# Two pools instead of one behind the attention, other low words on GpSimd, and another port rule and other priorities in the planner

## Chip, cores and metric

The kernel runs on one core of one Trainium2 chip. The metric is the device time of one execution in microseconds (us): the median of several runs. An engine is named as in the profile: PE is TensorE, DVE VectorE, ACT ScalarE, POOL GpSimd, SP the queue that issues most DMAs.

## What is computed

```python
# q, k, v: (4, 8, 768, 64); proj (64, 6)
bucket = sum(((x @ proj) > 0) * 2**j)            # of every q row and k row
scores = where(q_bucket == k_bucket, 0.125 * q @ k.T, -1e9)
attn   = exp(scores - max) ; attn /= attn.sum + 1e-9 ; out = attn @ v
x = out with the 8 heads side by side             # (4, 768, 512)
h = gelu(x @ w_in)                                # (4, 768, 1024), tanh form
u, v = h[..., :512], h[..., 512:]
v_n = (v - mean) / sqrt(var + 1e-6) * g_ln
v_s = w_sg @ v_n + b_sg
out = x + (u * v_s) @ w_out
```

The weights w_in, w_sg and w_out come as 64-bit floats; the kernel makes 32-bit words of them. All large products run as three matmuls over a high and a low word of each factor.

## The kernel before

**Attention.** Sixteen pairs (a batch and two heads) are worked through in halves of 384 queries, 32 halves in all. `prepare` transposes q and k and makes the bucket features (PE lines 491 and 511, DVE 498 and 514). `largest` computes scores for the row maxima (PE L531), which DVE reduces (`mx`, L536, six reductions to a half); `shift` brings the maxima into the features. `weigh` computes the scores again (PE L569), ACT takes the exponentials into a ring of eight tiles `p` (L573), and POOL adds them up into `sum` (L586, ten additions of 128x384 to a half). `weighted` multiplies them with v (PE L597, 24 matmuls). `finish` sends the sums through four small DMAs to get reciprocals, scales, and stores the half's x to DRAM (`xs`).

**Input weights.** `weight_job` turns a piece of 128x256 of w_in into words: one POOL product (L369), and on DVE the operations of lines 367, 368, 370, 372, 373, 374, then an ACT copy (L375) and a DVE subtraction (L376). Sixteen such jobs are spread over the attention, by the priority `WSTEP * i + WP`. The same function makes the output weights `woh`, `wol` later, in sixteen pieces of 128x128 with one set of buffers (`ow`, `owx`, `owy`, `owg`).

**The gMLP.** For each batch: `load_x` fetches x and splits it (ACT L700, POOL L698). `hidden_v` is 72 matmuls (L765) into six PSUM banks, a gelu on ACT and DVE (L749, L750, L752, L754), the norm (L772 to L775), the scaling (L777), the high word `zh` on ACT (L779) and the low word `zl` on DVE (L781); its result `y` has two buffers. `hidden_u` is 96 matmuls (L797) and a gelu. `gate` is 144 matmuls (L815), then L818, L822, L823 and on POOL L826. `project` is 72 matmuls (L841) and a transpose for the residual (L846). Batch 0's `hidden_v` runs inside the last attention halves. Between batch 0's `hidden_u` and its `gate`, the gate weights are loaded on the ACT queue (b_sg at L707, six loads of w_sg at L716, 384 KB each), transposed on PE (L724), and split on ACT (L730) and DVE (L733).

**What sets the order.** `Plan` collects all operations with a cost and a priority and works out an order by a list schedule over engines, PSUM banks and DMA lanes; `run` then emits the instructions in that order, and each engine takes its own in order. Its `port` rule holds back operations of DVE and POOL that are marked as users of a shared port: after one starts, none of either engine is planned before its end. Memory comes from pools on a left and a right stack. Left are `late`, `odd`, `even`, `early` (attention). `b3` on the right (gate weights, output weights, `u`, `gs`, and the small tiles `gt`, `rx`, `ob`) is opened when all four are closed, the finishing steps of the last half among them.

Of the kernel before, what the change touches and what calls it, by code (L numbers as in the profile page):

```python
# [9 lines left out]
F32 = mybir.dt.float32  # L10
F32R = mybir.dt.float32r
# [10 lines left out]
MLP = {"xl": "POOL", "gm": "DVE", "gl": "POOL", "wg": 434.12, "wo": 12.91, "x": 469.98}  # L22

HID = 260.1
AVP = 2.39
S0P = 1.18
AHEAD = 4
PREP, SHIFTP, FINP, WSTEP, WP = 5.65, -1.32, 4.0, 37.92, -61.79
# [4 lines left out]
class Plan:  # L33
# [5 lines left out]
    WAIT = 0.2  # L39
    SOON = 0.11  # L40
# [38 lines left out]
    def add(self, engine, cost, prio, fn, r=(), w=(), dma=0, port=None, form=None, lat=0.0):  # L79
# [4 lines left out]
        for kind, xs in (("r", r), ("w", w)):  # L84
            for x in xs:
# [23 lines left out]
    def order(self):  # L109
# [14 lines left out]
        port, form = 0.0, None  # L124

        def since(n):
            e = G[n]["e"]
            if G[n]["dma"]:
                return max(seq.get(e, 0.0), lanes[-self.LANES] if len(lanes) >= self.LANES else 0.0)
            return max(free[e], seq.get(e, 0.0), port if G[n]["port"] and not G[n]["dma"] else 0.0)  # L130
# [11 lines left out]
        while len(out) < len(G):  # L142
# [53 lines left out]
            else:  # L196
                free[e] = end
                if g["port"]:
                    port = end
# [32 lines left out]
def kernel(  # L232
# [103 lines left out]
    def weight_job(plan, tile_of, src, c, f0, CW, th, tl, fac, prio):  # L336
# [14 lines left out]
        ops = iter(range(1, 12))  # L351

        def when():
            i = next(ops)
            return prio

        def vec(fn, r, wr):
            plan.add("DVE", 0.07 + CW / 960.0, when(), fn, r, wr, port=True)

        def vec2(fn, r, wr):  # L360
            plan.add("DVE", 0.07 + CW / 1920.0, when(), fn, r, wr, port=True)

# [4 lines left out]
        vec2(lambda: V.tensor_scalar(y(), hi(), 3, 0x3FFFFFFF, op0=ALU.logical_shift_left, op1=ALU.bitwise_and), [w], [y])  # L367
        vec(lambda: sts(x(), hi(), -0x40000000, y(), op0=ALU.bitwise_and, op1=ALU.bitwise_or), [w, y], [x])  # L368
        plan.add("POOL", 0.14 + CW / 512, when(), lambda: nc.gpsimd.tensor_mul(g(), hi().bitcast(F32), hi().bitcast(F32)), [w], [g])  # L369
        vec(lambda: sts(xf(), g(), LEAST * LEAST, xf(), op0=ALU.is_ge, op1=ALU.mult), [x, g], [x])  # L370

        vec2(lambda: V.tensor_single_scalar(y(), x(), -0x800000, op=ALU.bitwise_and), [x], [y])
        vec(lambda: sts(yf(), lo().bitcast(U32), 2.0 ** -52, yf(), op0=ALU.mult, op1=ALU.mult), [w, y], [y])
        vec(lambda: V.tensor_add(xf(), xf(), yf()), [x, y], [x])
        plan.add("ACT", 0.06 + CW / 1300, when(), lambda: nc.scalar.mul(part(th), xf(), fac), [x], [d] + bufs[:1])  # L375
        vec(lambda: sts(part(tl), xf(), fac, part(th).bitcast(F32), op0=ALU.mult, op1=ALU.subtract),  # L376
            [x, d] + bufs[:1], bufs[1:])
# [5 lines left out]
    MEM = "MEM"  # L383
    xd = [[plan.buf(f"xd_{b}_{c}", 1) for c in range(NC)] for b in range(B)]
# [36 lines left out]
    late, odd, even, early = (Pool(n, "left") for n in ("late", "odd", "even", "early"))  # L421
# [7 lines left out]
    if True:  # L429
# [22 lines left out]
        ptiles = [late.pool.tile([P, 2, SH + 1], F32, tag=f"p{i}", name=f"p{i}", bufs=1) for i in range(NPT)]  # L452
# [3 lines left out]
        def p_tile():  # L456
            late.list.append(plan.buf("p", NPT, lambda i: ptiles[i % NPT]))
            return late.list[-1]
# [450 lines left out]
```

## Time and profile before

| | us |
|---|---|
| median of 3 runs | 815.61 |
| lowest, highest | 812.11, 815.83 |
| the profiled execution, its own time | 815.91 |
| its span, first to last instruction | 814.1 |

A busy PE in the profile is a PE with a matmul in its pipeline. Waits are put down to what released them last. The granted clock of PE is 1.00 at 2.4 GHz and 0.50 at 1.2 GHz; a number between is a mean over a stretch. Instruction shapes are partitions x elements.

### The profile page before, as it was taken

What the parts mean: (1) busy time and instruction counts of PE and PEld (TensorE: products, weight loads), DVE (VectorE), ACT (ScalarE), POOL (GpSimd) and SP (SyncE); (2) the same over time, 40 slices, a digit from 0 to 9 for tenths busy, and PEclk for the clock granted to TensorE, in tenths of its full rate; (3) what the DMA queues carried; (4) which work ended last, traced back from release to release, by engine and by line L of the source; (5) the groups of instructions that cost most, each with busy time, mean ns of one, the idle gap of its engine ahead of it and who ended that gap; (6) DMA issues with size and microseconds to landing.
All of it is one profiled execution on the core that took longest, in us unless ns stands there. A gap on an engine that the chain in (4) does not pass through costs nothing.

```text
span 814.1 us, 14589 instructions
## 1 busy us (share of the span) xinstructions
PE 772.9 (95%) x5480; PEld 614.5 (75%) x5480; DVE 553.7 (68%) x918; ACT 403.5 (50%) x702; POOL 427.9 (53%) x466
## 2 busy tenths in 40 slices
PE   4979999999999999999999999599899999999998
PEld 3657667776767676776767669489898889988996
DVE  7986876877668769779677556698982158407730
ACT  2345656666566556665666565524432136214411
POOL 1465878787887777877877753233232202401130
PEclk9989999999999999999999999799999999999999
DMA  8003441432244224313311011610124220030003
GB/s 206 15 27 80 121 105 53 125 98 67 84 110 103 69 54 115 89 46 101 89 42 40 31 30 51 219 46 20 46 73 153 93 66 20 21 128 28 1 0 130
DMA packets 99302, 60.89 MB, mean 75 GB/s; under 512 B 64288, under 2 KB 91040, under 8 KB 99232
## 3 DMA queue, kind: packets, MB, share of 16 engines
q1 hardware_dynamic: 97920, 56.94, 25.3%
q10 hardware_dynamic: 1312, 3.02, 1.1%
q8 instruction: 43, 0.70, 0.4%
q14 instruction: 27, 0.22, 0.1%
HBM read 47.16 MB, written 12.78 MB: 74 GB/s over the span
## 4 chain that ended last, share of the span: by engine, by line
PE 80%; DVE 14%; DMA 2%; issue 2%; ACT 1%; POOL 0%; SPq 0%; ACTq 0%; DVEq 0%
PE psb L597 15%; PE psb L569 14%; PE psb L815 10%; PE psb L841 8%; PE psb L531 8%; PE psb L765 7%; PE psb L797 6%; PE psb L511 4%; DVE mx L536 4%; PE psb L491 3%; PE psb L612 1%; PE psb L846 1%; PE psb L549 1%; DVE wy L367 1%; DVE owx L368 1%
## 5 line engine op out<-in xcount | busy, mean ns | idle before, releaser
L586 POOL TENSOR_TENSOR sum<-sum,p 128x384 f32<-128x384 f32 x256 | 239.8, 969 | 10.6 <-ACT p L573 10.6
L536 DVE TENSOR_REDUCE mx<-psb 128x2 f32<-128x768 f32 x192 | 174.1, 949 | 62.3 <-PE psb L531 59.0
L573 ACT ACTIVATE p<-psb 128x768 f32<-128x768 f32 x192 | 146.5, 812 | 71.6 <-PE psb L569 68.5
L597 PE MATMUL psb<-p,v 128*64 128x385 f32 x768 | 133.5, 498 | 0.0
L597 PEld LDWEIGHTS psb<-p,v 128*64 128x64 f32 x768 | 52.9, 138 | 64.8 <-issue 62.0
L586 POOL TENSOR_TENSOR sum<-p,p 128x384 f32<-128x384 f32 x64 | 64.1, 1022 | 36.9 <-ACT p L573 36.6
L531 PE MATMUL psb<-fk,fq 64*128 64x384 f32 x384 | 72.8, 374 | 4.5 <-DVE mx L536 1.7
L569 PE MATMUL psb<-hq,hk 64*128 64x384 f32 x384 | 69.6, 356 | 5.3 <-DVE mx L536 4.6
L750 DVE SCALAR_TENSOR_TENSOR h<-h,psb 128x384 f32<-128x384 f32 (+1 forms) x56 | 32.6, 604 | 60.8 <-ACT h L749 60.6
L826 POOL TENSOR_TENSOR gs<-gt,gs 128x384 fp32r<-128x384 f32 x32 | 33.5, 1052 | 76.2 <-ACT gs L823 75.8
L775 POOL TENSOR_TENSOR mv<-mv,epsr 128x1 f32<-128x1 f32 x24 | 14.1, 587 | 106.0 <-DVE mv L774 101.1
L815 PE MATMUL psb<-wgh,zh 128*128 128x384 f32 x192 | 65.3, 340 | 4.4 <-DVE u L754 3.0
L841 PE MATMUL psb<-woh,gs 128*128 128x512 f32 x192 | 65.5, 402 | 0.0
L531 PE MATMUL psb<-hk,hq 64*128 64x384 f32 x384 | 65.3, 335 | 0.0
L569 PE MATMUL psb<-fq,fk 64*128 64x384 f32 x384 | 65.3, 334 | 0.0
L569 PE MATMUL psb<-hq,lk 64*128 64x384 f32 x384 | 65.2, 333 | 0.0
L569 PE MATMUL psb<-lq,hk 64*128 64x384 f32 x384 | 65.2, 333 | 0.0
L815 PE MATMUL psb<-wgl,zh 128*128 128x384 f32 x192 | 64.7, 337 | 0.0
L815 PE MATMUL psb<-wgh,zl 128*128 128x384 f32 x192 | 64.7, 337 | 0.0
L633 POOL TENSOR_TENSOR xt<-xt,e 128x384 f32<-128x384 f32 x32 | 32.5, 1014 | 57.1 <-ACT e L631 32.7
L531 PEld LDWEIGHTS psb<-fk,fq 64*128 64x128 f32 x384 | 36.1, 184 | 32.0 <-issue 15.8
L818 DVE TENSOR_TENSOR gt<-psb,b_bc 128x384 f32<-128x384 f32 x32 | 17.7, 554 | 48.9 <-PE psb L815 31.2
(125 smaller groups left out, 1685.2 us busy)
## 6 DMA issues: line engine op xcount, KB each, us to landing
q<-in_q_dram SPq DMA_DIRECT2D x32, 192.0 KB
k<-in_k_dram SPq DMA_DIRECT2D x32, 192.0 KB
v<-in_v_dram SPq DMA_DIRECT2D x16, 384.0 KB
rs<-r SPq DMA_DIRECT2D x64, 96.0 KB
xs<-xt SPq DMA_DIRECT2D x32, 192.0 KB
x<-xs SPq DMA_DIRECT2D x16, 384.0 KB
rx<-xs SPq DMA_DIRECT2D x96, 64.0 KB
out_dram<-ob SPq DMA_DIRECT2D x24, 256.0 KB
```

Of the source, the lines that this page charges most:

```text
L531: nc.tensor.matmul(sc[kh]()[:, j, :SH], x[0]()[row(j), qs], x[1]()[row(j), kh * SH:(kh + 1) * SH], start=(n == 0), stop=(n == 1))
L536: plan.add(DVE, 0.95, prio, lambda kh=kh: nc.vector.tensor_reduce(mx()[:, kh, i, :], sc[kh]()[:, :, :SH], axis=AX.X, op=ALU.max, negate=Tr ...
L569: nc.tensor.matmul(sc[i]()[:, j, :SH], x()[row(j), ks], y()[row(j), cs], start=(n == 0), stop=(n == 3))
L573: plan.add(ACT, 0.81, prio, lambda i=i: nc.scalar.activation(p[i]()[:, :, :SH], sc[i]()[:, :, :SH], AF.Exp), [sc[i]], [p[i]])
L586: plan.add(POOL, 1.03, prio + 0.6, lambda i=i, j=j, first=first: nc.gpsimd.tensor_add(sums()[:, j], (first or sums)()[:, j, :SH], p[i]()[: ...
L597: nc.tensor.matmul(av()[row(j), :SH + 1], st.v()[:, j, kt, :], p[kt]()[:, j, :], start=(kt == 0), stop=(kt == NT - 1))
L750: plan.add(DVE, us + 0.07, prio, lambda: nc.vector.scalar_tensor_tensor(h2()[:, :n], h2()[:, :n], 1.0 / GA, ps()[:, :n], op0=ALU.add, op1= ...
L765: nc.tensor.matmul(ps(), x()[:, ts_], w[:, c, FH:FF], start=(c == 0 and n == 0), stop=(c == NC - 1 and n == 2))
L797: nc.tensor.matmul(ps()[:, :SH], w[:, c, fs], x()[:, cs], start=(c == 0 and n == 0), stop=(c == NC - 1 and n == 2))
L815: nc.tensor.matmul(vp()[:, :SH], z()[:, t, fs], w()[:, t, cs], start=(t == 0 and n == 0), stop=(t == NT - 1 and n == 2))
L826: nc.gpsimd if e == POOL else nc.vector).tensor_sub(gl()[:, cs], gt(), gh()[:, cs].bitcast(F32)),
L841: nc.tensor.matmul(po(), a()[:, ts_], w()[:, f, :], start=(f == 0 and n == 0), stop=False)
```

## The change

The tiles `p`, `sum` and `v` move from `late` to a new pool `held`, which is closed together with `odd`, `even`, `early`. In their place `b3` is opened, now with the gate weights, `b_bc`, `gs` and `u` alone; a second pool `b4` holds the output weights and the rest, and is opened when `late` is closed too. In `weight_job`, the output weights' addition and their low word go to POOL, and ACT makes the word in two passes. In `hidden_v`, `zl` is made by POOL from a scaled `y`, with one more ACT pass. The port rule keeps one time for each engine: an operation of DVE holds POOL until 0.25 us before its end, one of POOL holds DVE until 0.2 us before its end. The matmuls on w_in now have the conversion as a dependency in the plan. Costs and priorities are other numbers.

```diff
-MLP = {"xl": "POOL", "gm": "DVE", "gl": "POOL", "wg": 434.12, "wo": 12.91, "x": 469.98}
-HID = 260.1
+MLP = {"xl": "POOL", "gm": "DVE", "gl": "POOL", "wg": 463.45, "wo": -43.61, "x": 464.83}
+HID = 277.32
...
-PREP, SHIFTP, FINP, WSTEP, WP = 5.65, -1.32, 4.0, 37.92, -61.79
+PREP, SHIFTP, FINP, WSTEP, WP = 4.15, -4.68, 2.34, 48.11, -68.38
...
+    LOCK_DVE, LOCK_POOL = 0.2, 0.25
...
                 if g["port"]:
-                    port = end
+                    if e == "POOL":
+                        port["DVE"] = end - self.LOCK_DVE
+                    else:
+                        port["POOL"] = end - self.LOCK_POOL
...
+        if bufs:
+            plan.add("POOL", 0.14 + CW / 512, prio, lambda: nc.gpsimd.tensor_add(xf(), xf(), yf()), [x, y], [x])
+            plan.add("ACT", 0.16 + CW / 1300, prio, lambda: nc.scalar.mul(xf(), xf(), fac), [x], [x])
+            plan.add("ACT", 0.16 + CW / 1300, prio, lambda: nc.scalar.copy(part(th), xf()), [x], [d] + bufs[:1])
+            plan.add("POOL", 0.14 + CW / 512, prio, lambda: nc.gpsimd.tensor_sub(part(tl), xf(), part(th).bitcast(F32)),
+                     [x, d] + bufs[:1], bufs[1:])
+            return
...
-            plan.add(ACT, 0.72, p0, lambda y=y, mv=mv, t=t: nc.scalar.mul(zh()[:, t, :], y(), mv()[:, 2:3]),
-                     [y, mv], [(zh, t)])
-            plan.add(DVE, 0.76, p0, lambda y=y, mv=mv, t=t: V.scalar_tensor_tensor(
-                zl()[:, t, :], y(), mv()[:, 2:3], zh()[:, t, :].bitcast(F32), op0=ALU.mult, op1=ALU.subtract),
-                [y, mv, (zh, t)], [(zl, t)], port=True)
+            plan.add(ACT, 0.72, p0, lambda y=y, mv=mv: nc.scalar.mul(y(), y(), mv()[:, 2:3]), [y, mv], [y])
+            plan.add(ACT, 0.62, p0, lambda y=y, t=t: nc.scalar.copy(zh()[:, t, :], y()), [y], [(zh, t)])
+            plan.add(POOL, 1.35, p0, lambda y=y, t=t: nc.gpsimd.tensor_sub(zl()[:, t, :], y(), zh()[:, t, :].bitcast(F32)),
+                     [y, (zh, t)], [(zl, t)])
...
-    end = odd.close(even.close(early.close()))
-    end = late.close(end)
+    end = held.close(odd.close(even.close(early.close())))
     b3 = Pool("b3", "right", None, end)
+    place_of.update(gs=b3, u=b3)
...
+    b4 = Pool("b4", "right", None, late.close(end) + [b3.need])
+    woh, wol = b4.ring([P, NF, DM], F32R, "woh"), b4.ring([P, NF, DM], F32R, "wol")
```

The order moves in three places that matter below. Line numbers of the changed kernel are 9 higher in the attention (L536 is L545, L543 is L552), and 367, 368, 370, 372, 373, 374, 376 of a w_in job are 370, 371, 372, 374, 375, 383, 385.

DVE in the first pair, where conversions (names `w`, `wx`, `wy`) stand among the row maxima; before:

```order
L536 TENSOR_REDUCE mx_516<-psb 128x2 x3
L543 SCALAR_TENSOR_TENSOR m_108<-mx_432 128x6
L376 SCALAR_TENSOR_TENSOR wil<-wx_355,wih 128x256
L367 TENSOR_SCALAR wy_541<-w_3_411 128x256
L368 SCALAR_TENSOR_TENSOR wx_543<-w_3_411,wy_541 128x256
L370 SCALAR_TENSOR_TENSOR wx_543<-wg_444,wx_543 128x256
L372 TENSOR_SCALAR wy_541<-wx_543 128x256
L373 SCALAR_TENSOR_TENSOR wy_541<-w_3_411,wy_541 128x256
L374 TENSOR_TENSOR wx_543<-wx_543,wy_541 128x256
L536 TENSOR_REDUCE mx_516<-psb 128x2 x3
```

and after:

```order
L552 SCALAR_TENSOR_TENSOR m_108<-mx_435 128x6
L545 TENSOR_REDUCE mx_520<-psb 128x2 x4
L385 SCALAR_TENSOR_TENSOR wil<-wx_359,wih 128x256
L370 TENSOR_SCALAR wy_556<-w_3_418 128x256
L371 SCALAR_TENSOR_TENSOR wx_569<-w_3_418,wy_556 128x256
L372 SCALAR_TENSOR_TENSOR wx_569<-wg_456,wx_569 128x256
L374 TENSOR_SCALAR wy_556<-wx_569 128x256
L375 SCALAR_TENSOR_TENSOR wy_556<-w_3_418,wy_556 128x256
L383 TENSOR_TENSOR wx_569<-wx_569,wy_556 128x256
L385 SCALAR_TENSOR_TENSOR wil<-wx_569,wih 128x256
L545 TENSOR_REDUCE mx_520<-psb 128x2 x2
```

The block comes one reduction later. Before, a second block of seven follows three reductions on, and the later halves have 2, 5, 7 and 0 conversion operations among their six reductions, in turn; after, no other whole job stands in one piece, and the halves from the fourth on have 3 to 5 each, until the conversions end in half 23 (before: half 30).

ACT at the end of the attention, where the gate weights' DMAs (`gs`) are issued; before:

```order
L631 ACTIVATE e_5895<-e_5895,vm_5661 128x384
L700 CAST xh_5909<-x_2456 128x768
L700 CAST xh_5915<-x_2793 128x768
L707 DMA gs_5931<-in_moe_b_sg_dram 128x768
L716 DMA gs_5937<-in_moe_w_sg_dram 128x768
L749 ACTIVATE h_8_5945<-psb 128x384
L716 DMA gs_5947<-in_moe_w_sg_dram 128x768
L749 ACTIVATE h_9_5950<-psb 128x384
L716 DMA gs_5952<-in_moe_w_sg_dram 128x768
L716 DMA gs_5958<-in_moe_w_sg_dram 128x768
L752 ACTIVATE h_8_5945<-h_8_5945 128x384
L752 ACTIVATE h_9_5950<-h_9_5950 128x384
```

and after (`un` is the last half's product leaving PSUM, `sm` its sums; L758 and L761 are L749 and L752, L725 is L716):

```order
L626 COPY un_5673<-psb 128x385
L638 ACTIVATE vm_5678<-un_5673 128x1
L758 ACTIVATE h_2_5687<-psb 128x512
L624 ACTIVATE sm_5699<-psb,tiny 128x192
L716 DMA gs_5705<-in_moe_b_sg_dram 128x768
L761 ACTIVATE h_2_5687<-h_2_5687 128x512
L725 DMA gs_5714<-in_moe_w_sg_dram 128x768
L725 DMA gs_5718<-in_moe_w_sg_dram 128x768
L725 DMA gs_5726<-in_moe_w_sg_dram 128x768
L788 ACTIVATE y_5663<-y_5663,mv_5675 128x512
L725 DMA gs_5732<-in_moe_w_sg_dram 128x768
```

The seven loads move from behind batch 0's `hidden_u` to behind the last half's sums, by 33 L765 and 96 L797 of PE; the two that are not shown follow within seven more rows.

POOL in the stretch of the output weights (`owg`, `owx`, `wol`) and of batch 1's `xl`; before:

```order
L698 TENSOR_TENSOR xl_5920<-x_2456,xh_5909 128x768
L698 TENSOR_TENSOR xl_5923<-x_2793,xh_5915 128x768
L369 TENSOR_TENSOR owg_5970<-ow_0_5935 128x128
L698 TENSOR_TENSOR xl_5999<-x_5925,xh_5973 128x768
L369 TENSOR_TENSOR owg_6075<-ow_1_6001 128x128
L698 TENSOR_TENSOR xl_6104<-x_6053,xh_6093 128x768
```

and after:

```order
L707 TENSOR_TENSOR xl_5967<-x_2466,xh_5957 128x768
L368 TENSOR_TENSOR owg_6017<-ow_0_5983 128x128
L377 TENSOR_TENSOR owx_6024<-owx_6024,owy_6019 128x128
L707 TENSOR_TENSOR xl_6046<-x_2807,xh_6034 128x768
L380 TENSOR_TENSOR wol_6070<-owx_6024,woh_6049 128x128
L368 TENSOR_TENSOR owg_6076<-ow_1_6037 128x128
L377 TENSOR_TENSOR owx_6084<-owx_6084,owy_6079 128x128
L707 TENSOR_TENSOR xl_6106<-x_6053,xh_6095 128x768
L380 TENSOR_TENSOR wol_6070<-owx_6084,woh_6049 128x128
```

Each job now passes POOL three times, with an `xl` between the second and the third pass of the first jobs.

PE's own matmuls are the same ones. Around the last attention half its order was: the last 24 L597, 48 L765, 96 L797, then 30 L765 among 36 L724, and L815. It is now: the last 24 L597, 42 L765, 96 L797, 36 L724, 15 L765, 144 L815, 57 L765, 96 L797 (batch 1), 123 L815 (batch 1), and the first projection. Before, the first projection came after 144 L815, 42 L765, 96 L797 and 93 L815.

## Rows read from the trace of the kernel before

**Rows 1.** Windows by stage: busy us of PE, PEld, DVE, ACT, POOL; clock, DMA share, GB/s

```profile
36.00:60.00 24.00, 19.64 (x142) 12.04 (x140) 21.07 (x27) 9.88 (x17) 18.67 (x19) 0.86 0.07 23
60.00:473.00 413.00, 405.66 (x3506) 293.11 (x3503) 307.29 (x397) 256.50 (x430) 317.73 (x337) 1.00 0.31 80
473.00:506.40 33.40, 33.40 (x179) 27.91 (x178) 23.13 (x45) 17.37 (x31) 12.57 (x16) 1.00 0.11 31
506.40:536.30 29.90, 19.78 (x85) 15.24 (x84) 21.34 (x52) 15.37 (x34) 8.42 (x8) 0.83 0.56 181
536.30:586.00 49.70, 49.06 (x264) 46.51 (x264) 45.31 (x120) 17.59 (x35) 15.91 (x23) 1.00 0.08 25
586.00:607.50 21.50, 18.44 (x96) 17.79 (x96) 20.47 (x40) 9.30 (x20) 8.63 (x7) 0.92 0.28 92
607.50:814.00 206.50, 202.97 (x1059) 182.91 (x1058) 85.27 (x165) 65.93 (x121) 38.83 (x40) 1.00 0.20 63
```

**Rows 2.** PE's waits over the whole span: total us, times, longest

```profile
PE psb L724 <- DVE u L754: 7.7, 4, 3.7
PE psb L569 <- DVE mx L536: 4.6, 3, 2.6
PE psb L511 <- DVE mx L536: 3.7, 4, 1.2
PE psb L815 <- DVE u L754: 3.0, 1, 3.0
PE psb L491 <- DVE mx L536: 2.0, 2, 1.6
```

**Rows 3.** Timeline of DVE in the first pair: start, us, instruction

```profile
42.38 0.29 DVE L372 TENSOR_SCALAR wy<-wx 128x256 int32<-128x256 int32 x1
49.69 1.00 DVE L372 TENSOR_SCALAR wy<-wx 128x256 int32<-128x256 int32 x1
```

**Rows 4.** Timeline of PE there, idle time before it in brackets

```profile
53.75 0.69 PE L569 MATMUL psb<-hq,hk 64*128 64x384 f32 x2 [2.61 <-DVE mx L536]
```

**Rows 5.** The chain that ended last, around the attention's end: start, us

```profile
473.62 4.03 PE psb L597 x24
...
507.79 5.32 DMA x<-xs
...
514.58 0.55 DVE u L754
```

**Rows 6.** The same chain in batch 2, where PE runs without a gap

```profile
654.81 16.74 PE psb L765 x72
671.55 16.90 PE psb L797 x96
688.44 24.96 PE psb L815 x144
```

**Rows 7.** Timeline of PE among the gate weights' transposes

```profile
515.19 0.93 PE L724 MATMUL psb<-ident,gs 128*128 128x128 f32 x3 [3.71 <-DVE u L754]
...
527.63 1.80 PE L724 MATMUL psb<-ident,gs 128*128 128x128 f32 x9 [0.90 <-DVE u L754]
```

**Rows 8.** Groups of POOL and DVE from 536.3 to 607.5: total us, mean ns

```profile
L698 POOL TENSOR_TENSOR xl<-x,xh 128x768 fp32r<-128x768 f32 x4 | 7.5, 1868 | 6.3 <-ACT xh L700 6.3
L369 POOL TENSOR_TENSOR owg<-ow 128x128 f32<-128x128 f32 x12 | 5.2, 435 | 7.3 <-DMA ow<-in_moe_w_out_dram 7.3
...
L781 DVE SCALAR_TENSOR_TENSOR zl<-y,mv,zh 128x512 fp32r<-128x512 f32 x6 | 4.4, 742 | 0.0
L376 DVE SCALAR_TENSOR_TENSOR wol<-owx,woh 128x128 fp32r<-128x128 f32 x12 | 3.6, 298 | 0.0
```

**Rows 9.** Timeline of DVE and POOL: one operation alone, and behind POOL

```profile
576.26 0.29 DVE L374 TENSOR_TENSOR owx<-owx,owy 128x128 f32<-128x128 f32 x1
586.35 1.77 DVE L374 TENSOR_TENSOR owx<-owx,owy 128x128 f32<-128x128 f32 x1
...
586.11 1.86 POOL L698 TENSOR_TENSOR xl<-x,xh 128x768 fp32r<-128x768 f32 x1 [0.92 <-ACT xh L700]
```

More of the change, by code (lines that the diff above doesn't have):

```diff
@@ L123, in order @@
         free, seq, ready, dma_free, pe, till, lanes = {}, {}, {}, 0.0, {}, {}, []
-        port, form = 0.0, None
+        port, form = {"DVE": 0.0, "POOL": 0.0}, None
         def since(n):
@@ L129, in since @@
                 return max(seq.get(e, 0.0), lanes[-self.LANES] if len(lanes) >= self.LANES else 0.0)
-            return max(free[e], seq.get(e, 0.0), port if G[n]["port"] and not G[n]["dma"] else 0.0)
+            return max(free[e], seq.get(e, 0.0), port[e] if G[n]["port"] and not G[n]["dma"] else 0.0)
         def when(n):
@@ L346, in weight_job @@
         sts = V.scalar_tensor_tensor
+        if bank is not None:
+            z = bank()
+            yi, yf, zf = (lambda: z()[:, :CW].bitcast(I32)), (lambda: z()[:, :CW]), (lambda: z()[:, CW:2 * CW])
+            port, y, o = False, z, z
+        else:
+            y = tile_of([P, CW], I32, "wy")
+            yi, yf, zf = y, (lambda: y().bitcast(F32)), (lambda: x().bitcast(F32))
+            port, o = True, x
         def load():
             nc.sync.dma_start(w().rearrange("p a b -> p (a b)"), src[c * P:(c + 1) * P, f0:f0 + CW].bitcast(I32))
-        ops = iter(range(1, 12))
@@ L367, in weight_job @@
[L367 to L372, printed above, removed]
@@ L373, in weight_job, with vec @@
-        vec(lambda: sts(yf(), lo().bitcast(U32), 2.0 ** -52, yf(), op0=ALU.mult, op1=ALU.mult), [w, y], [y])
[L374 to L377, printed above, removed]
+        def vec(fn, r, wr, fast=False):
+            plan.add("DVE", 0.16 + CW / (1920.0 if fast and port else 960.0), prio, fn, r, wr, port=port)
@@ L379 @@
+        vec(lambda: V.tensor_add(zf(), xf(), yf()), [x, y], [o])
+        plan.add("ACT", 0.16 + CW / 1300, prio, lambda: nc.scalar.mul(part(th), zf(), fac), [o], [d] + bufs[:1])
+        vec(lambda: sts(part(tl), zf(), fac, part(th).bitcast(F32), op0=ALU.mult, op1=ALU.subtract), [o, d] + bufs[:1], bufs[1:] + ([(mark, (c, f0))] if mark else []))
     PE, DVE, ACT, POOL, SP = "PE", "DVE", "ACT", "POOL", "SP"
@@ L420 @@
     setup.release()
-    late, odd, even, early = (Pool(n, "left") for n in ("late", "odd", "even", "early"))
+    late, held, odd, even, early = (Pool(n, "left") for n in ("late", "held", "odd", "even", "early"))
     if True:
@@ L451 @@
         NPT = 8
-        ptiles = [late.pool.tile([P, 2, SH + 1], F32, tag=f"p{i}", name=f"p{i}", bufs=1) for i in range(NPT)]
+        ptiles = [held.pool.tile([P, 2, SH + 1], F32, tag=f"p{i}", name=f"p{i}", bufs=1) for i in range(NPT)]
         for i, t in enumerate(ptiles):
@@ L456, in p_tile @@
         def p_tile():
-            late.list.append(plan.buf("p", NPT, lambda i: ptiles[i % NPT]))
-            return late.list[-1]
+            held.list.append(plan.buf("p", NPT, lambda i: ptiles[i % NPT]))
+            return held.list[-1]
         def row(j):
@@ L659 @@
         for i, job in enumerate(wjobs):
-            weight_job(plan, w_tile, *job, WSTEP * i + WP)
+            weight_job(plan, w_tile, *job, WSTEP * i + WP, BANKED and ps_one or None, win)
         prepare(0)
@@ L766, in mm @@
                                          stop=(c == NC - 1 and n == 2))
-                plan.add(PE, 0.696, p0 + 0.01 * c, mm, [xh, xl], [ps])
+                plan.add(PE, 0.696, p0 + 0.01 * c, mm, [xh, xl] + [(win, (c, f0)) for f0 in range(FH, FF, CW)], [ps])
             y = tile_of([P, FH], F32, "y", 2)
@@ L876 @@
     plan.run(tc)
-    for p in (b3, b2, b1, ps_s):
+    for p in (b4, b3, b2, b1, ps_s):
         p.pool.release()
```

39 lines of the change are left out of this document (18 added, 21 removed).

## Prediction

> **What bounds the kernel now.** I read the windows by stage first, because the share of PE over the whole span hides where it stands still. The window from 607.5 us on [rows 1] has PE busy in 202.97 of 206.5 us at full clock, with DVE at 85 and POOL at 39: batches 2 and 3 are bound by PE, the 3.5 us left are the end, and the change takes no matmul away, so nothing is to be had there. The losses lie in three places. (a) The attention: from 36 to 60 us PE is idle for 24.0 - 19.64 = 4.4 us and its mean clock is 0.86, which is 0.14 x 24 = 3.4 us more; from 60 to 473 it is idle for 413 - 405.66 = 7.3 us. Together 15.1 us. (b) The passage from batch 0's `hidden_u` to its gate, 506.4 to 536.3: idle for 10.1 us and a clock of 0.83. (c) 586 to 607.5: idle for 3.1 us, clock 0.92.
>
> PE's waits say who is late [rows 2]: always DVE. In (a) it is the row maxima (4.6, 3.7 and 2.0 us behind `mx`), in (b) the gelu of `hidden_u`, which gives its PSUM banks back late (7.7 us in four waits of the transposes), in (c) the same for batch 1 (3.0 us).
>
> **(a) Conversions among the row maxima.** A conversion of a w_in piece takes DVE 0.29 us when it runs alone and 1.00 us while POOL adds up exponentials [rows 3]: it waits for the running POOL operation. A whole job in one piece then takes DVE six to seven microseconds, the maxima behind it come late, and PE stands for 2.61 us [rows 4] and drops to its lower level afterwards. The new order has one such piece of eight in place of two of seven, and behind one more reduction, so that PE has the 24 products of a half (4.03 us [rows 5]) and score tiles in hand; the later halves carry 3 to 5 conversions instead of 2, 5, 7 and 0 in turn. No conversion is saved, only their bunching. I put the gain at 5 of the 7.8 us before 60 us and 3.5 of the 7.3 behind it: **-8.5**. The bounds are 15.1, all of it, and 0, if the steady load only spreads the same waits.
>
> **(b) The passage.** What PE must do there at full clock is priced from batch 2 and from one clean run of transposes: 16.74/72 = 0.233 us for an L765, 16.90/96 = 0.176 for an L797, 24.96/144 = 0.173 for an L815 [rows 6], 1.80/9 = 0.2 for a transpose L724 [rows 7]. The window holds 30 L765, 36 L724 and 18 L815: 7.0 + 7.2 + 3.1 = 17.3 us of work in 29.9, so 12.6 us are lost. The chain shows how: a load of batch 1's x lands 5.32 us after its issue, beside the gate weights; only then can ACT, which has the gate weights' DMA issues in its queue, go on to the tanh, and DVE's `u` comes at 514.58 [rows 5]. PE's banks are full till then: 3.71 us before the first transpose [rows 7].
>
> In the new order ACT issues these seven loads right behind the last half's sums, ahead of 33 L765 and 96 L797 (7.7 + 16.9 = 24.6 us of PE). They have 2.75 MB, some 14 us at the rate of this window (181 GB/s [rows 1], the last figure), and so land before the transposes. Queued behind these issues on ACT are the gelu of batch 0's third row tile and after; each issue of the seven costs ACT less than an activation, and PE has its banks' worth of work meanwhile: I take nothing for it. The DMAs of the last half's `finish`, SP's, now run beside these loads. If each of the four hops came 2 us later, the last `xt` product on DVE would hold up the gelu behind it by up to 8 us, but those banks are wanted only some 25 us after the sums: nothing, with a bound of 4.
>
> What is late next is DVE. From the end of `hidden_u` to the last low word of the gate weights it has 12 subtractions and 6 gelu steps of 0.55 us (as the `u` of [rows 5]), 11 steps of the output weights of 0.29 [rows 9], and one wait for an `xl` of POOL of 1.87 [rows 8]: 6.6 + 3.3 + 3.2 + 1.9 = 15.0 us. PE has 36 x 0.2 + 15 x 0.233 = 10.7. So 4.3 of the 12.6 us stay: **-8.3**. The bounds are -12.6 and 0.
>
> **(c) GpSimd instead of VectorE.** A job of the output weights loses on DVE an addition (0.29 [rows 9]) and a subtraction (0.298 [rows 8]) and gains on POOL two operations like L369 (0.435 [rows 8]); ACT gets a second pass, on an engine that is busy for a third of the window. A `zl` takes DVE 0.742; on POOL, by width from `xl`, 1.868 x 512/768 = 1.25. Between the first gate matmul and the first projection there are 13 jobs and 6 `zl`. DVE is relieved of 13 x 0.59 + 6 x 0.74 = 12.1 us, where it is busy for 65.8 of 71.2 us now [rows 1]; but POOL gets 13 x 0.87 + 6 x 1.25 = 18.8 us more beside the 24.5 it has. All of these operations keep to one port: DVE's L374 takes 1.77 us instead of 0.29 when it meets an `xl` of 1.86 [rows 9]. Port time rises by 18.8 - 12.1 = 6.7 us, and PE's own work in the stretch is 25.0 + 57 x 0.233 + 16.9 + 123 x 0.173 = 76.5 us, against 71.2 taken now. DVE has more room, its port less; the loss of 3.1 us and the clock's 1.7 (0.08 x 21.5) could go or double. I take **0**, between -4.8 and +6.7.
>
> The Trainium skill, page "SBUF — State Buffer", section "Who interferes with whom", has a rule that speaks against this part: the port pair which VectorE and GpSimd share is taken as a whole for an instruction's length, and the other engine is blocked until it ends, also for a VectorE operation with two SBUF inputs. The trace agrees (the 1.77 us of [rows 9]). By that rule work moved to the slower engine makes the pair busier, which is the third rival.
>
> In batches 2 and 3 `zl` on POOL costs nothing as long as PE is the bound: POOL is busy for 39 of 206 us and needs 7.5 us more to a batch. Its cover is `hidden_u`, 16.9 us. `y` has two buffers and is held longer, till POOL has read it; if that cover were gone, each batch would lose what a late `zl` takes, some 1.25 us.
>
> The pools by themselves cost nothing and move no instruction on the chip; they allow the plan to put the loads earlier.
>
> **Sum.** The profiled execution took 815.9 us (span 814.1 and 1.8 around it), 0.3 above the median of 815.6. 815.9 - 8.5 - 8.3 + 0 = **799.1 us**.
>
> **Rivals.** 1. *Only one of two holds.* If the maxima come as late as before, 815.9 - 8.3 = 807.6. If the passage stays, 807.4: then the change doesn't do what its pools are for, since the loads' issues would wait on ACT for older DMAs to land, as ACT waits now. Against it: in front of them stand only the sums and their small DMAs.
>
> 2. *The chain of the output weights becomes the bound, slower than before.* All sixteen pieces use one set of buffers, so a job must have passed POOL a third time before the next writes `owx`. Now twelve low words are made in 71.2 us [rows 8], 5.9 us to a job; after, 13 jobs have 76.5 us, 5.9 again. Alone a job would take five DVE steps of 0.29, two POOL steps of 0.435 and two ACT passes no longer than those: about 2.9 us. But the new order puts an `xl` of 1.87 us between POOL's steps, and if a job meets three such waits it takes 2.9 + 5.6 = 8.5. Each 0.1 us over 5.9 delays the first projection by 1.3 us, so from 7.2 us to a job on the gain of 16.8 is gone. At 7.7 it is 13 x 1.8 = 23.4 us: 799.1 + 23.4 = 822.5. For it: in-order queues and a port that is nearly always taken. Against it: after the first three jobs all `xl` of batch 1 are done, and batch 2's come with the last ones.
>
> 3. *The port takes back what DVE gains.* The 6.7 us of port time land on PE, and the 4 us bound of the late finish too, and half of (a) stays: 799.1 + 6.7 + 4 + 4.2 = 814.0.
>
> **How the numbers follow.** The forecast 0.55 (788 to 807), one of two 0.20 (807 to 810), the port 0.10 (810 to 818), the chain of the output weights 0.12 (816 to 830), more than all this 0.03 (below 787: 815.9 - 15.1 - 12.6 - 4.8 = 783.4 if every loss went). Half a per cent, 4.1 us, is about what a measurement of this kernel can tell from no change, so faster means below 811.5. Faster has the forecast, the first rival and the last case, 0.78, less a little of the first rival's upper end: 0.77; same 0.10; slower 0.13. The range from 786 to 815 leaves out the slower rival and part of the third.
>
> **What would show it.** (a) right: PE idle from 36 to 60 us below 2 us at a clock near 1, and waits behind `mx` below 5 us in all (10.3 in the three rows now); wrong: single waits over 2 us elsewhere in the first pairs. (b) right: no wait over 2 us of the transposes, the seven loads issued before batch 0's `hidden_u`, and ACT not idle between `hidden_u` and the gate; some 4 us of waiting by DVE's low words. Wrong: ACT's issues stand apart by landings, or the first gate matmul comes later than 46 us behind the last L597. (c) right: low words of the output weights 6 us apart or closer, and no wait of the first L841; wrong: L841 waits for POOL's `wol`. The prediction falls as a whole if PE is idle in batches 2 and 3.

## The result

The changed kernel takes 793.4 us (median of four runs, 792.9 to 794.5) against 815.7 before: a ratio of 0.973, interval 0.970 to 0.977. The profiled execution took 793.26 us, 22.6 less than the one before. The forecast was 799.1.

To see where the 22.6 us come from, I cut each profiled execution at PE's own marks. *Attention* ends with the last matmul of `weighted` (L597 before, L606 after), less 0.2325 us for each w_in matmul done by then. *Passage* runs from there to the first gate matmul, *third* from there to the first projection, *rest* is what follows. In the passage and in the third stretch, *work* is what PE's matmuls cost at the rates of [rows 6, 7], and *lost* is the remainder, idle time and low clock together. The *rest* ends with PE's last matmul.

| us | attention | passage: took, work, lost | third: took, work, lost |
|---|---|---|---|
| before | 472.1 | 54.5, 42.7, 11.7 | 75.2, 67.7, 7.5 |
| after | 461.5 | 41.3, 37.8, 3.5 | 80.2, 76.4, 3.8 |
| gain | 10.6 | 8.2 | 3.7 |
| forecast | 8.5 | 8.3 | 0 |

The rest, less its matmuls of `hidden_v`, `hidden_u` and `gate`, is 76.8 us before and 76.7 after.

The windows by stage of the changed kernel (us; busy us of PE, PEld, DVE, ACT, POOL; clock, DMA share, GB/s) answer [rows 1]:

```profile
36.00:60.00 24.00, 24.00 (x220) 16.93 (x216) 19.61 (x28) 13.51 (x25) 18.84 (x21) 1.00 0.27 67
60.00:468.50 408.50, 406.03 (x3462) 289.15 (x3458) 319.17 (x403) 256.17 (x429) 329.11 (x343) 1.00 0.31 79
468.50:509.80 41.30, 37.16 (x197) 32.94 (x198) 31.07 (x69) 29.72 (x61) 22.44 (x25) 1.00 0.44 133
509.80:590.10 80.30, 78.46 (x422) 75.52 (x421) 59.39 (x141) 36.06 (x80) 47.21 (x66) 0.98 0.15 50
590.10:791.40 201.30, 197.72 (x1030) 177.75 (x1028) 77.62 (x148) 74.18 (x132) 55.84 (x52) 1.00 0.20 65
```

The stretch from 36 to 60 us has no idle time and full clock (it had lost 7.8 us); behind it 2.5 us of idle time are left of 7.3. The last line is bound by PE as before: POOL has its 17 us more there and nobody waits.

PE's waits (total us, times, longest) answer [rows 2]. The first and the third are the passage's, the second is the third stretch's; the last two are the largest behind `m` and `mx` in the attention:

```profile
PE psb L733 <- DVE u L763: 2.2, 1, 2.2
PE psb L805 <- DVE y L763: 1.8, 1, 1.8
PE psb L774 <- DVE wgl L742: 1.7, 1, 1.7
...
PE psb L558 <- DVE m L552: 2.4, 7, 0.4
PE psb L540 <- DVE mx L545: 1.7, 3, 1.2
```

The waits behind `m` are what is left from 36 us on. Those of the last row lie before 23 us, and the kernel before has them too (L531, 1.7 us in three); of the three `mx` rows of [rows 2], 10.3 us, one wait of 0.3 is left, before 24 us.

### The profile page after: what moved, and what is told of

It is laid out like the page before. It is cut to its first block, busy times and chain, and to the rows that moved or that the text cites. A ratio compares the mean times of both kernels' runs of the same rounds, so it can differ in the third digit from the quotient of the medians.

```text
span 791.5 us, 14719 instructions
## 1 busy us (share of the span) xinstructions
PE 767.8 (97%) x5480; PEld 613.0 (77%) x5480; DVE 536.9 (68%) x862; ACT 421.1 (53%) x742; POOL 481.0 (61%) x522
## 4 chain that ended last, share of the span: by engine, by line
PE 86%; DVE 8%; DMA 2%; ACT 1%; issue 1%; POOL 0%; DVEq 0%; ACTq 0%; POOLq 0%; SPq 0%
PE psb L578 16%; PE psb L606 16%; PE psb L823 13%; PE psb L540 10%; PE psb L849 8%; PE psb L774 6%; PE psb L805 5%; PE psb L520 5%; PE psb L500 2%; DVE mx L545 2%; PE psb L621 2%; PE psb L558 2%; PE psb L854 1%; DVE m L552 1%; DMA sq<-s 1%
## 5 line engine op out<-in xcount | busy, mean ns | idle before, releaser
L595 POOL TENSOR_TENSOR sum<-sum,p 128x384 f32<-128x384 f32 x256 | 243.6, 983 | 8.4 <-ACT p L582 8.4
L545 DVE TENSOR_REDUCE mx<-psb 128x2 f32<-128x768 f32 x192 | 174.7, 952 | 63.1 <-PE psb L540 61.8
L606 PE MATMUL psb<-p,v 128*64 128x385 f32 x768 | 131.2, 491 | 0.0
L606 PEld LDWEIGHTS psb<-p,v 128*64 128x64 f32 x768 | 52.3, 137 | 64.0 <-issue 62.8
L784 POOL TENSOR_TENSOR mv<-mv,epsr 128x1 f32<-128x1 f32 x24 | 14.1, 588 | 67.8 <-DVE mv L783 67.7
L626 ACT COPY un<-psb 128x385 f32<-128x385 f32 x32 | 15.5, 483 | 68.2 <-PE psb L606 68.2
```

Source lines behind the costliest of these rows:

```text
L545: plan.add(DVE, 0.95, prio, lambda kh=kh: nc.vector.tensor_reduce(mx()[:, kh, i, :], sc[kh]()[:, :, :SH], axis=AX.X, op=ALU.max, negate=Tr ...
L595: plan.add(POOL, 1.03, prio + 0.6, lambda i=i, j=j, first=first: nc.gpsimd.tensor_add(sums()[:, j], (first or sums)()[:, j, :SH], p[i]()[: ...
L606: nc.tensor.matmul(av()[row(j), :SH + 1], st.v()[:, j, kt, :], p[kt]()[:, j, :], start=(kt == 0), stop=(kt == NT - 1))
```

## The experiments

All stage numbers below are from the profiled execution of each kernel, cut as above. In each group the kernel before ran on the same chip; ratios are to that. The changed kernel itself ran only for the result, so times are set beside its 793.4 across groups.

### One part undone in the changed kernel

The kernel before had a median of 814.4 us here. By ratio to it the four kernels below stand 2 to 3 us above the changed kernel, and the intervals of the ratios (some 0.006 either way) overlap with that one's; the stages are the firmer evidence.

First, the pools put back (what `held` holds returns to `late`, and `b4` is `b3`), so that the gate weights are loaded behind `hidden_u` again:

```diff
-    late, held, odd, even, early = (Pool(n, "left") for n in ("late", "held", "odd", "even", "early"))
+    late, odd, even, early = (Pool(n, "left") for n in ("late", "odd", "even", "early"))
+    held = late
...
-    end = held.close(odd.close(even.close(early.close())))
+    end = late.close(odd.close(even.close(early.close())))
...
-    b4 = Pool("b4", "right", None, late.close(end) + [b3.need])
+    b4 = b3
```

> The changed kernel with its pools put back: p, sum and v in late, one pool b3 behind all of the attention, all else as changed. The plan then puts the seven loads behind batch 0's hidden_u again. Theory (the early loads made the passage short): the first gate matmul comes some 8 us later after the last L606 than in the changed kernel, with waits of over 2 us of the transposes behind the gelu, and the attention is the same; 793.4 + 8 = 801 us. Rival (VectorE's relief made the passage short, the pools little): under 3 us lost, 793 to 796.

Measured 796.9 us (794.2 to 797.6), ratio 0.977. That is 3.4 above the changed kernel: not the theory's 8, and a little over the rival's 3. The profiled execution was the fastest of the four; in it the passage lost 6.4 us instead of 3.5, and 1.6 came back in the third stretch. The gate weights' issues were late, but ScalarE did not stand still between them as it had before. Timelines of ACT's queue in the kernel before (first two lines), then of ACT's and SP's queues in this one (start, us, instruction):

```profile
513.13 0.85 ACTq L716 DMA_DIRECT2D gs<-in_moe_w_sg_dram  x2
514.02 0.52 ACT L752 ACTIVATE h<-h 128x384 f32<-128x384 f32 x1 [6.63 <-DMA x<-xs]
```

```profile
494.61 0.93 ACTq L726 DMA_DIRECT2D gs<-in_moe_w_sg_dram  x2
495.61 0.41 ACTq L726 DMA_DIRECT2D gs<-in_moe_w_sg_dram  x1
...
502.02 1.30 SPq L705 DMA_DIRECT2D x<-xs  x2
```

Before, ACT's third w_sg issue came only when batch 1's x load had landed (507.79 + 5.32 = 513.11 [rows 5]), and the tanh behind it with it, after 6.63 us of idle time. In this kernel SP issues that x load behind the first output weights and `rx`, at 502.02, and five w_sg issues pass at once. So the order of SP's loads, not the pools, had taken the stall away here; the second group asks which part moved it.

Next, the output weights' addition and low word back on VectorE (the branch `if bufs:` with its `return` is taken out):

```diff
-        if bufs:
-            plan.add("POOL", 0.14 + CW / 512, prio, lambda: nc.gpsimd.tensor_add(xf(), xf(), yf()), [x, y], [x])
...
-            return
```

> The changed kernel with the output weights' addition and low word back on VectorE. Theory (VectorE is the late one between the first gate matmul and the first projection, and its relief is what counts): the waits of batch 1's hidden_u and of the gate behind VectorE grow, 2 to 5 us lost, 795 to 798. Rival (the shared port takes back what VectorE gains, since two of three operations are slower on GpSimd): no loss or a gain of up to 4 us, 789 to 793.

Measured 796.6 us (795.8 to 797.2). And v's low word back on VectorE, from `y` and the factor as before:

```diff
-            plan.add(POOL, 1.35, p0, lambda y=y, t=t: nc.gpsimd.tensor_sub(zl()[:, t, :], y(), zh()[:, t, :].bitcast(F32)),
-                     [y, (zh, t)], [(zl, t)])
+            plan.add(DVE, 0.76, p0, lambda y=y, mv=mv, t=t: V.scalar_tensor_tensor(
+                zl()[:, t, :], y(), mv()[:, 2:3], zh()[:, t, :].bitcast(F32), op0=ALU.mult, op1=ALU.subtract),
+                [y, mv, (zh, t)], [(zl, t)], port=True)
```

> The changed kernel with the low word of normalised v back on VectorE. Theory as for the output weights, with 6 x 0.74 us to a batch: 1 to 4 us lost, all of it before the first projection, and no idle PE in batches 2 and 3; 794 to 797. Rival (port, and y held longer by GpSimd): a gain of 1 to 4 us, 789 to 792.

Measured 795.5 us (794.6 to 797.4). Each of the two is worth 2 to 3 us, as the theory said, and the port rival is out: nothing became faster with the work back. (Either edit also takes one ACT pass away.) In the third stretch 5.4 and 8.1 us were lost instead of 3.8. PE's waits there, first of the kernel with the output weights on VectorE, then of the one with v's low word:

```profile
PE psb L798 <- DVE y L756: 3.2, 1, 3.2
```

```profile
PE psb L806 <- DVE y L763: 2.7, 1, 2.7
PE psb L824 <- DVE u L763: 2.0, 2, 1.1
```

It is the gelu, queued on DVE behind the moved operations, that gives PE's banks back late.

Last, the old port rule (one time for both engines, no early release):

```diff
-                    if e == "POOL":
-                        port["DVE"] = end - self.LOCK_DVE
-                    else:
-                        port["POOL"] = end - self.LOCK_POOL
+                    port = end
```

> The changed kernel with the planner's old port rule, one time for both engines. Theory (the numbers for the conversions, not the rule, spread the attention's load): the last L606 starts within 2 us of the changed kernel's 464.4 and the time is 792 to 797. Rival (the rule does it): the last L606 starts 4 us or more later, waits behind the row maxima of over 1 us come back, 797 to 803.

Measured 795.4 us (795.1 to 795.6). The attention ended at 464.1, 2.6 later, between the theory's 2 and the rival's 4; the passage lost 1.8 more, and 2.4 came back in the third stretch, which lost 1.4 only. The attention's windows (columns as above):

```profile
36.00:60.00 24.00, 24.00 (x214) 17.08 (x213) 19.43 (x27) 14.44 (x25) 18.96 (x21) 1.00 0.27 70
60.00:471.00 411.00, 402.59 (x3455) 290.01 (x3453) 305.12 (x397) 253.53 (x426) 320.88 (x340) 1.00 0.29 78
```

The loss before 60 us stays away without the rule; the idle time behind it is 8.4 us, as much as before the change. In the changed kernel the rule is what takes that away (2.5 left), though the end moves by less than the difference. And it does so late: the first `weighted` of the eighth half starts at 131.3 us here and at 131.5 with the rule (141.2 before), and the delay comes behind 250 us.

### One part alone in the kernel before

On this chip the kernel before spread from 812 to 824 us (median 820.6), in two bunches; so I read stages, and give each profiled span beside 814.1, which is from the lower bunch.

| us | span | attention | passage lost | third lost |
|---|---|---|---|---|
| before | 814.1 | 472.1 | 11.7 | 7.5 |
| attention numbers alone | 813.8 | 466.0 | 13.7 | 11.3 |
| pools alone | 808.1 | 471.5 | 5.4 | 8.6 |
| x load later alone | 816.2 | 476.1 | 8.7 | 8.5 |
| low words alone | 813.6 | 476.4 | 7.8 | 6.7 |

```diff
-HID = 260.1
-AVP = 2.39
-S0P = 1.18
+HID = 277.32
+AVP = 3.21
+S0P = 0.22
...
-PREP, SHIFTP, FINP, WSTEP, WP = 5.65, -1.32, 4.0, 37.92, -61.79
+PREP, SHIFTP, FINP, WSTEP, WP = 4.15, -4.68, 2.34, 48.11, -68.38
```

> The kernel before with the changed kernel's numbers of the attention alone (HID, AVP, S0P, PREP, SHIFTP, FINP, WSTEP, WP); old port rule, old pools, low words on VectorE. Theory: the numbers by themselves make the attention shorter by about 8 us (the changed kernel with the old port rule had lost 2.6 of its 10.6), so with the passage and the third stretch as before about 806 to 809, and a last L597 some 8 us earlier once the L765 before it are taken off. Rival: numbers and rule only work together; then the attention gains 4 or less, 811 to 815.

Median 819.0 us, ratio 0.999 (0.996 to 1.002). The attention did get 6.1 us shorter (8 in the theory), and everything came back: 2.0 us more lost in the passage, 3.8 in the third stretch. The windows say which part of the attention the numbers mend:

```profile
36.00:60.00 24.00, 22.66 (x202) 15.44 (x202) 16.35 (x25) 12.30 (x22) 18.50 (x21) 1.00 0.10 29
60.00:473.70 413.70, 406.08 (x3477) 293.05 (x3475) 317.12 (x410) 257.25 (x431) 322.60 (x341) 1.00 0.31 80
```

1.3 us are idle before 60 us, with full clock, instead of 7.8 lost; behind it 7.6, as before. So the bunching of conversions was the loss at the start, and the numbers alone mend 6.5 of the 7.8.

Next, the pools alone, the edits of the first experiment the other way round:

> The kernel before with the two pools of the changed kernel alone; the seven gate weight loads move ahead of hidden_u, all else of the change is left out. Theory: before, ScalarE stood for 5.5 us because its third w_sg issue had to wait until the x load landed; with the loads early that stall cannot come, and the passage loses 4 to 5 us instead of 11.7: 807 to 809. Rival: the pools are worth only the 3 us that their undoing cost in the changed kernel: 811 to 813.

Median 809.8 us (808.1 to 810.7), ratio 0.989 (0.985 to 0.992), just above the theory's range. The seven loads went out from 483.3 to 488.1 us, and the passage lost 5.4 us. Here the pools are worth 6.3 us in the passage, twice what their undoing cost: the stall was still there to be cured.

Then batch 1's x loads behind a piece of the gate weights, with nothing else changed:

```diff
-            dma(prio + c, 1.09, lambda eng, x=x, c=c: eng.dma_start(x(), xs[b][c]), [xd[b][c]], [x])
+            dma(prio + c, 1.09, lambda eng, x=x, c=c: eng.dma_start(x(), xs[b][c]),
+                [xd[b][c]] + ([(wgh, (1, 0))] if b == 1 else []), [x])
```

> The kernel before with one more dependency: batch 1's x loads come behind a piece of the gate weights, and so behind the w_sg issues instead of among them. The loads stay late, behind hidden_u. Theory (the stall of ScalarE's queue on the x load's landing): no idle time of ScalarE of over 3 us between the w_sg issues, the passage loses 5 to 7 us instead of 11.7: 808 to 811. Rival (VectorE's work or the seven loads' own time makes the loss): the passage stays within 2 us, 813 to 817.

Median 819.2 us, ratio 1.001 (0.997 to 1.006). The passage lost 8.7 us instead of 11.7, short of what the theory wanted. The x load is out of the way, but ACT's queue still stands from 506.6 to 509.2 us ahead of its second w_sg issue, and another 1.28 us that are put down to a load of the output weights:

```profile
505.18 0.44 ACTq L717 DMA_DIRECT2D gs<-in_moe_w_sg_dram  x1
506.07 0.49 ACT L750 ACTIVATE h<-psb 128x384 f32<-128x384 f32 x1 [0.65 <-DVE u L755]
509.20 0.36 ACTq L717 DMA_DIRECT2D gs<-in_moe_w_sg_dram  x1
...
511.42 0.52 ACT L753 ACTIVATE h<-h 128x384 f32<-128x384 f32 x1 [1.28 <-DMA ow<-in_moe_w_out_dram]
```

The trace's semaphore events name the first one too: the issue at 509.20 waits for a semaphore that was last raised at 509.18, by the landing of ACT's own b_sg load, issued at 504.80. The x load was one case of several. So the stall on x is about 3 us of the passage's loss, and the loads' lateness, with these other landings, another 3 (8.7 here, 5.4 with the pools). This execution also has a wait of 4.5 us in the attention that the profile of before doesn't show; it stands in the last section.

Then the low words on GpSimd alone (both edits of the first group the other way round):

> The kernel before with the low words of v and of the output weights on GpSimd alone; old pools, rule and numbers. In its order SP issues batch 1's first x load behind the output weights and rx, not ahead of them. Theory: that takes the stall out of the passage (5 to 6 us) and VectorE's relief takes 2 to 4 us from the third stretch: 804 to 808. Rival, the prediction's port sum: no gain in the passage and 0 to 6.7 us more in the third stretch: 814 to 821.

Median 815.8 us, ratio 0.997 (0.994 to 1.001). The passage lost 7.8 us: in this plan too SP issues x behind the output weights and `rx`, and ACT sends five w_sg issues from 510.2 to 513.4 without a stall. So it was the low words that had moved the x load. The third stretch lost 6.7 us, neither the theory's gain nor the port's loss. One wait makes it: PE stands 4.08 us, and its granted clock is 0.50 for 6.8 us from 584.3 on (timelines of PE and DVE):

```profile
586.27 0.69 PE L803 MATMUL psb<-xh,wih 128*128 128x384 f32 x1 [4.08 <-DVE u L761]
```

```profile
583.41 0.29 DVE L367 TENSOR_SCALAR owy<-ow 128x128 int32<-128x128 int32 x1
...
585.01 0.74 DVE L784 SCALAR_TENSOR_TENSOR y<-y,mv,g_bc 128x512 f32<-128x512 f32 x1
585.67 0.55 DVE L761 SCALAR_TENSOR_TENSOR u<-h,psb 128x384 f32<-128x384 f32 x1
```

The gelu `u` stands on DVE behind a whole job and a norm. Low words on GpSimd give DVE room; whether PE gets it depends on the order that the numbers make.

### Combinations

The kernel before had a median of 819.6 us here.

The attention's numbers and the port rule together (with the plan's dependency of the w_in matmuls on the conversions), old pools, low words on VectorE:

> The kernel before with the changed kernel's attention numbers, its port rule and the plan's dependency of the w_in matmuls on the conversions; old pools, old MLP numbers, low words on VectorE. The numbers alone had shortened the attention by 6.1 us, which came back later. Theory: numbers and rule add up, so the last L597 (less the w_in matmuls before it) comes 8.5 to 10.6 us earlier, and since batch 1's x load again stands ahead of rx on SP, ScalarE's queue stalls again behind it and the passage loses 10 us or more: 808 to 812. Rival: the rule alone makes the attention gain no larger (6 us or less), or the passage is cured by it as well: 800 to 806.

830.3 us (830.1 to 830.8), ratio 1.014 (1.009 to 1.018): slower than before, which neither theory had. The attention ended at 483.8, 11.7 us late, though PE was idle for no longer than before. Windows of the same 100 us, first of this kernel, then of the changed one:

```profile
300.00:400.00 100.00, 96.18 (x794) 65.99 (x792) 59.88 (x72) 56.37 (x93) 66.50 (x71) 0.98 0.26 65
```

```profile
300.00:400.00 100.00, 98.96 (x853) 71.25 (x853) 68.59 (x85) 59.78 (x100) 75.22 (x81) 1.00 0.29 72
```

Nearly as busy, with 59 matmuls fewer. The timeline of PE shows why busy time hides it: matmuls start 0.17 us apart and last 0.34, so a wait of 0.1 us leaves no gap.

```profile
325.14 0.33 PE L536 MATMUL psb<-fk,fq 64*128 64x384 f32 x2
325.32 0.34 PE L536 MATMUL psb<-hk,hq 64*128 64x384 f32 x2
325.58 0.45 PE L536 MATMUL psb<-fk,fq 64*128 64x384 f32 x2
```

From 36 us on, the 708 matmuls of L536 take 85.9 us from start to next start, and 73.7 in the kernel before. Up to 150 us one takes 0.108 us here, behind that 0.126 (0.104 before, on either side). Whose results they wait for the trace doesn't say for waits so short. But it says when the time went. The first `weighted` of a half starts at (us):

| half | 8th | 16th | 24th | 32nd |
|---|---|---|---|---|
| before | 141.2 | 252.6 | 364.3 | 473.5 |
| numbers and rule | 131.7 | 253.1 | 373.5 | 488.1 |
| changed | 131.5 | 241.5 | 352.2 | 464.4 |

Up to the eighth half numbers and rule have the changed kernel's whole lead; behind it they fall back, to an end of the attention 22.3 us later (483.8 for 461.5). At 153.91 the plan has put the first tile of batch 0's `hidden_u` among the scores, twelve matmuls that end at 185.3, and nothing reads a tile of `hidden_u` before 506.27 (timelines of PE and ACT):

```profile
153.91 0.45 PE L802 MATMUL psb<-xh,wih 128*128 128x384 f32 x1
...
184.53 0.44 PE L802 MATMUL psb<-xh,wih 128*128 128x384 f32 x1
```

```profile
506.27 0.47 ACT L754 ACTIVATE h<-psb 128x384 f32<-128x384 f32 x1
```

The gelu of this tile writes `u`, in `b3`, which opens only when the attention's pools are closed. So one of the eight PSUM banks stays taken for over 350 us, while `largest` and `weigh` each ask for two pairs of banks, of which there are four. No other kernel here runs `hidden_u` before 455 us. That this tile is the cause fits the time at which the loss begins; no run took it out, so it is not shown. Nor does this run show that numbers and rule are no gain by themselves: in the first quarter, ahead of that tile, they are one.

The kernel before once more, for the two bunches of its times:

> The kernel before itself, one more profile. In the last group its times fell into two bunches, 812 to 816 and 819 to 824, and two kernels with its order of the attention showed one wait of 4.55 us near 205 us, with L543 on VectorE taking 5.59 us while GpSimd made seven additions in a row. Theory: if this execution is above 818.5, that wait is there; if it is below 816.5, L543 takes under 1.2 us everywhere. Rival: a time above 818.5 without such a wait, or a wait with a time below 816.5; then the bunches have another cause.

815.4 us, from the lower bunch, with no such wait and the same stages as before (attention 471.6, 12.0 and 7.2 lost). The upper bunch was not caught.

The changed kernel with the old MLP numbers:

```diff
-MLP = {"xl": "POOL", "gm": "DVE", "gl": "POOL", "wg": 463.45, "wo": -43.61, "x": 464.83}
+MLP = {"xl": "POOL", "gm": "DVE", "gl": "POOL", "wg": 434.12, "wo": 12.91, "x": 469.98}
```

> The changed kernel with the old MLP numbers (gate weights, output weights and x later or earlier in the plan); attention, pools, low words and rule stay. Theory: since the loads are early and x stands behind rx either way, these numbers are worth little: 792 to 796. Rival: the third stretch's gain of 3.7 us is theirs: 797 to 798.

792.2 us (791.9 to 792.8), ratio 0.967 (0.963 to 0.970). These numbers are worth nothing in the change; the stages are those of the changed kernel (3.5 and 3.4 lost). It may be 1 us faster, but the changed kernel was not run beside it, and the intervals of the ratios touch.

Last, HID as changed and the other attention numbers as before (AVP, S0P and the line of PREP in the first diff of the second group):

> The changed kernel with HID as it is and the other attention numbers as before; the plan then puts batch 0's hidden_v and hidden_u between the score tiles of the last twenty halves. Theory: TensorE gets work where it waited, but VectorE gets 18 gelu steps among the maxima, and waits come back there: 797 to 803. Rival: with hidden_u out of the passage its loss goes, and the whole is faster than the changed kernel: 788 to 792.

801.0 us (800.0 to 802.4). The attention ended at 466.0, with `hidden_u` partly inside it, and the third stretch lost 6.7 us: it is 8.8 us slower than the kernel ahead of it in this group, which has the changed kernel's stages. So, with HID kept, the fine numbers are worth some 8 us once rule, pools and low words are there, with what it costs that the plan now starts batch 0's `hidden_v` at 263 us.

## Why the prediction was right

**(a) The attention**, forecast 8.5, measured 10.6. The mechanism held: no idle time from 36 to 60 us, and no wait behind `mx` from there on where the three rows had 10.3 us (2.0 in two rows lie ahead of it). The term was mis-sized in both halves: all 7.8 us before 60 us went (5 forecast), and 4.8 of 7.3 behind (3.5). Of these 12.6 the end shows 10.6; half of the rest is that the first `weighted` starts 1.1 us later (37.3 for 36.2). What the prediction didn't separate, the runs separate in part. The numbers alone gave 6.1 of the 10.6, and the rule's undoing cost 2.6; the last 2 us belong to neither. Most of the gain is there early: the first `weighted` of the eighth half starts at 141.2 us before and at 131.5 after, at 136.8 with the numbers alone, at 131.7 with numbers and rule, and at 131.3 in the changed kernel without the rule. So up to there the rule isn't needed if the rest of the change is in. What in the rest does it is open: the plan's new costs for the conversions (on DVE a fixed 0.16 us in each where it was 0.07) were never tried alone. The prediction had given the rule no price at all.

**(b) The passage**, forecast 8.3, measured 8.2. The loads go out where the prediction put them, behind the last half's sums:

```profile
471.36 0.33 ACTq L716 DMA_DIRECT2D gs<-in_moe_b_sg_dram  x1
471.76 1.38 ACTq L725 DMA_DIRECT2D gs<-in_moe_w_sg_dram  x3
...
476.36 0.34 ACTq L725 DMA_DIRECT2D gs<-in_moe_w_sg_dram  x1
```

PE then waits 2.17, 0.26 and 1.67 us for DVE, 4.1 in all where 4.3 were forecast; the first gate matmul comes 41.3 us behind the last `weighted` (46 was the bound). One sign failed by a little: the 2.17 are a wait of the transposes, behind the gelu and not a low word, and none over 2 was to be there. (The loads' time was added up wrongly, too: 2.75 MB at 181 GB/s are 15 us, not 14; traffic falls off at about 482, 14 us ahead of the first transpose.)

The late `finish`, priced at nothing, was seen too: two of its hops took 4.82 and 5.95 us beside the loads, and DVE stood 1.54 us for the second. No matmul waited until 499.26. But the chain that ended last runs through both hops, DVE's queue and the low word that PE waits for at the end of the passage (pieces of the chain):

```profile
471.74 4.82 DMA s<-sm
476.58 5.95 DMA sq<-s
482.55 0.19 DVE sq L631
...
506.17 1.41 DVE wgl L742 x3
...
507.62 2.36 PE psb L774 x9
```

So that nothing was lost by them is not shown; they may hold part of the 3.5 us.

What was wrong in (b) is the sharing out: "the pools allow the plan to put the loads earlier" holds, but had the pools failed, rival 1's 807.4 would not have come, since the low words alone move batch 1's x load behind `rx` and cure half of it. The size was right partly because either cure does.

**(c) GpSimd instead of VectorE**, forecast 0, measured 3.7 gained, inside the bounds. The step that failed is the one that set the port's 6.7 us more against DVE's room, as if both were PE's time. The window of the same stretch of before:

```profile
532.10:607.40 75.30, 70.74 (x377) 67.19 (x376) 69.40 (x170) 28.95 (x58) 24.94 (x31) 0.98 0.15 47
```

DVE's idle time went from 5.9 to 20.9 us, POOL's busy time from 24.9 to 47.2. The prices were right (a `zl` 1.32 us for 1.25, a low word 0.49 for 0.435), and the port is felt:

```profile
L790 POOL TENSOR_TENSOR zl<-y,zh 128x512 fp32r<-128x512 f32 x6 | 7.8, 1315 | 0.8 <-ACT zh L789 0.8
L380 POOL TENSOR_TENSOR wol<-owx,woh 128x128 fp32r<-128x128 f32 x14 | 6.8, 486 | 5.6 <-ACT woh L379 5.6
...
L372 DVE SCALAR_TENSOR_TENSOR owx<-owg,owx 128x128 f32<-128x128 f32 x14 | 6.7, 480 | 1.1
```

L372 takes 0.48 us in the mean where it took 0.34. The stretch also had more to lose than the bounds said, 7.5 us and not 4.8. But what PE waits for in it is the gelu, which stands in DVE's queue; what stands on POOL is wanted only at the first projection, and comes in time: sixteen low words from 503.4 to 588.1 us, 5.6 apart (6 was the bound; rival 2 needed 7.2), and PE has no wait at 590. The rule of the Trainium skill that the prediction weighed, page "SBUF — State Buffer", section "Who interferes with whom", agrees with the trace: L372, which has two SBUF inputs, takes longer beside a busier POOL. The third rival that it stood behind didn't come, since the blocked operations weren't the ones waited for.

**The rest**: batches 2 and 3 lost nothing, as forecast. The forecast's 799.1 was 5.8 us too high, 2.1 from (a) and 3.7 from (c).

## What to carry to other kernels

An operation moved off an in-order queue is worth what stands behind it there, not the difference of the port or busy sums; ask whose results are urgent on either engine. A DMA issue on a compute engine's queue can wait for an older load to land, another queue's or its own (513.11 and 509.18 us above), and holds the activations behind it: look at the order in which the queues' loads go out together. Where a planner orders everything, undo a part *and* try it alone: here the pools were worth 3 us one way and 6 the other. And where a part alone does harm, ask at what time the loss begins, by the starts of the same step in each kernel, before calling the part worthless: numbers with rule were level with the whole change for a quarter of the attention and ended 12 us behind the kernel before.

## What the runs showed of the hardware

A short operation of DVE with two inputs in SBUF was held while POOL made seven in a row. In the kernel with the later x load, `m` (six columns, 0.26 us in the profile of before) started during the first of seven POOL additions and ended 0.02 us behind the last; PE stood 4.55 us. Timelines of DVE, POOL and PE:

```profile
204.05 5.59 DVE L543 SCALAR_TENSOR_TENSOR m<-mx 128x6 fp32r<-128x6 f32 x1
```

```profile
203.28 6.34 POOL L586 TENSOR_TENSOR sum<-sum,p 128x384 f32<-128x384 f32 x7
```

```profile
209.70 0.90 PE L549 MATMUL psb<-identr,m 128*128 128x128 f32 x3 [4.55 <-DVE m L543]
```

The kernel with the low words alone had the same 5.59 us at the same place. In the profile of before, `m` met six additions there and went in between:

```profile
207.78 0.26 DVE L543 SCALAR_TENSOR_TENSOR m<-mx 128x6 fp32r<-128x6 f32 x1
...
207.01 5.41 POOL L586 TENSOR_TENSOR sum<-sum,p 128x384 f32<-128x384 f32 x6
```

The Trainium skill, page "SBUF — State Buffer", section "Who interferes with whom", says that a VectorE instruction with two SBUF inputs contends with a GpSimd one that reads SBUF, for a port pair that is an exclusive lock. The common end agrees with that; if it was the lock, POOL was given it six times more while DVE stood ready. With the 6.8 us at a granted clock of 0.50 that followed, such a wait costs up to 8 us by my estimate (4.55 and half of 6.8), about the distance of the two bunches of before (812 to 816 and 819 to 824); that it makes them was not shown. None of the profiles of the changed kernel and its variants has one.
